# More zero products, pooled keys summed over rows, and a new order of steps in a fused attention and expert kernel

## The chip, the cores and the metric

One core of a Trainium2 chip. The metric is the device time of one execution in microseconds (us); times are medians of several runs.

## What is computed

```python
# attention: q, k, v of shape (2 batches, 8 heads, 576 tokens, 64)
out_d = sm_attn(mean of 4 tokens of q, of k, of v)        # pooled: 144 x 144 scores
out_local = softmax(q k^T / 8 where |i - j| < 4) v        # local band
x = (repeat(out_d, 4) + out_local) as 1152 tokens x 512
# experts: w1 (4, 512, 1024), w2 (4, 1024, 512)
p = domain_probs / sum(domain_probs)
out = sum over e of p[:, e] * (relu(x @ w1[e]) @ w2[e])
```

All of it is float32. The products of the experts are made of a high and a low part of each operand, three products for one.

## The kernel before

The work is cut into 1307 named steps. Each step belongs to one engine (P TensorE, V VectorE, A ScalarE, G POOL, S the load queue on SyncE), and a list written out by hand, ORDER, fixes the order in which the steps are issued. An engine does its steps strictly in that order. The dictionary ENGINE says for 133 small steps which engine does them.

Attention runs in four halves of a batch, a0 to a3, of 288 tokens each; a0 and a1 belong to the first batch. For a0, loads bring 72 x 1024 pieces of keys (k00n, k01n for the two halves of the keys), queries (q0n) and values (v00n, v01n), two loads of 288 KB each. `by_row` (k00r, q0r, k01r) reorders a piece on ScalarE or VectorE, `transposed` makes four transposes on TensorE for two heads (k00t.0 to .3, a0.qt.0 to .3, k01t.0 to .3) into one of three PSUM banks, and the steps k00te, a0.qte, k01te copy them out and free the bank. `pooled_bank` (L379 to L386, steps k00d, k01d) sums four tokens of the keys from the same bank on VectorE. The steps v00d and v01d sum the values on POOL in place.

Local attention has three blocks t in each half: a0.sc{t}.{0,1} are its scores (with products of `mask` ahead of them in a0), then max, sub, exp, sum, rec, norm on the small engines, blk (32 x 32 transposes on VectorE), pv (the product with the values), xs (sum with the pooled part), xh and xl (high and low part of x). Pooled attention goes by two pairs of groups g: ds (scores), dm (maximum), de (exponential), da, db (sum and reciprocal), dq (the share, on POOL in a0), dt (transposes), dc, dv. Its queries come from a0.qd, made on VectorE.

The first expert follows on the attention: m00 is its first 256 tokens, m00.m0 the first of eight groups of twelve products. It needs the x of all three blocks of a0 (a0.xl2 is the last) and a low part of the weights that POOL makes (wlo100). While m00 runs, attention a1 to a3 is woven into TensorE's queue; three more experts follow, with fewer products (sums of blocks in place of some of the products).

TensorE has 46 steps named warm, each with WARM[i] products of a 128 x 64 tile of zeros (`wz`) into a PSUM tile of their own (`wps`, L247), which nothing reads. Most of the 46 numbers are small or zero; their sum is 72.

Of the kernel before, what the change touches and what calls it, by code (L numbers as in the profile page):

```python
# [21 lines left out]
ORDER = """
    k00n.0 q0n.1 q0n.0 k00n.1 k00r.0 q0r.0 q0r.1 k00r.1 warm6 warm18 warm36 warm33 warm15 warm0 warm22 warm13 warm37
    warm21 warm40 k00t.0 warm11 warm29 k00t.1 warm2 warm41 warm19 warm23 a0.qt.2 warm42 a0.qt.0 warm34 a0.qt.1 warm16
    a0.qt.3 vw00 v01n.1 k01n.0 k01n.1 v00n.0 v00n.1 a1q.0 v01n.0 a1q.3 raw100 raw101 a1q.1 a1q.2 vw01 mask kstart0
    clear0 k00d.1 clear1 k00d.0 a0.start v01d.1 v00d.1 v01d.0 v00d.0 k00te.1 k00te.0 a0.qte.0 a0.qte.2 a0.qte.1
    a0.qd.0 warm27 k00t.3 k00d.3 warm5 warm17 k00t.2 k00te.3 k00te.2 a0.qte.3 a0.sc0.0 a0.sc0.1 warm12 a0.sc1.0 warm14
    a0.sc1.1 warm25 warm4 warm43 warm30 k01r.1 k00d.2 a0.qd.1 a0.max0 k01r.0 k01t.1 k01d.1 k01t.0 k01d.0 a0.max1
    a0.sub0 k01te.1 a0.sub1 k01t.2 k01d.2 warm3 a0.ds1 a0.ds0 a0.dm0 a0.dm1 k01te.0 a0.sc2.0 k01t.3 warm1 k01d.3 warm7
    a0.ds2 warm39 a0.exp0 a0.exp1 a0.de1 a0.de0 a0.da0 a0.sum1 k01te.2 a0.da1 a0.db1 a0.db0 a0.sum0 a0.dq0 a0.dt0  # L30
    warm9 a0.ds3 a0.dm2 a0.rec0 a0.dm3 k01te.3 a0.sc2.1 whi100.1 a0.dc0 a0.dq1 a0.max2 a0.de2 a0.sub2 a0.dt1 warm24
    warm28 warm38 a0.norm0 a0.da2 a0.dc1 a0.db2 a0.dq2 a0.de3 a0.exp2 a0.blk0.0 a0.da3 a0.db3 a0.blk0.1 a0.sum2
    a0.rec1 a0.dq3 a0.rec2 a0.norm1 wlo100.1 a0.blk1.1 a0.blk1.0 a0.norm2 a0.dv0 a0.dv1 a0.dt2 whi101.0 a0.dc2 a0.dt3
    a1.qt.1 warm44 a0.dv2 warm20 a0.dc3 a0.dv3 a0.pv0 whi101.1 whi100.0 a0.xd a0.xs0 a0.pv1 a1.qt.3 warm8 warm45
    warm31 a0.blk2.1 a0.blk2.0 vw02 a0.pv2 a1.qt.2 warm35 raw200 a0.xs1 k10r.3 praw raw201 k10r.2 k10r.1 a0.xh0 a0.xl0
    a1.start wlo100.0 a1.qte.1 a1.qte.3 wlo101.0 a0.xh1 whi200.1 a1.qte.2 a0.xs2 a1.qt.0 warm32 wlo101.1 whi200.0
    a0.xh2 a1.qte.0 a0.xl1 a0.xl2 a1.qd.0 a1.qd.1 warm26 a1.sc1.1 warm10 a1.sc0.1 a1.sc2.0 m00.m0 a1.ds0 a1.sc2.1
    m00.m2 m00.m3 a1.ds1 a1.dm0 m00.r0 a1.dm1 a1.madd2 wlo200.1 a1.de1 a1.de0 a1.da1 a1.da0 m00.l0 a1.sc0.0 a1.ds2
    wlo200.0 a1.db0 whi201.1 a1.dq0 a1.madd0 a1.dm2 a1.max2 a1.dt0 a1.sc1.0 a1.dc0 a1.db1 m00.r3 a1.de2 a1.da2 a1.ds3
    m00.m1 kstart1 a1.dq1 m00.r2 whi201.0 m00.r1 m00.l3 a1.max0 a1.dm3 m00.l1 a1.madd1 a1.db2 wlo201.1 a1.sub0 a1.sub2  # L40
    a1.dt1 a1.dv0 m00.m6 a1.dc1 k10r.0 m00.m4 k10t.2 a1.dv1 a1.de3 m00.r4 a1.exp0 a1.exp2 k11r.3 vw03 k11r.1 k11r.2
    vw04 vw05 k11r.0 v11n.1 v10n.1 a1.da3 a1.dq2 a1.dt2 a1.db3 m00.l2 a1.dq3 m00.m5 a1.dc2 a1.dt3 m00.o00 k10t.0
    m00.m7 a1.dc3 k10t.1 a1.dv3 a1.dv2 m00.r6 k10te.2 m00.l4 a1.sum0 wlo201.0 a1.max1 a1.sub1 a1.sum2 k11t.1 m00.o01
    m00.l6 a1.rec0 gate a1.rec2 a1.norm0 a1.blk0.0 a1.norm2 k10te.0 m00.r5 a1.exp1 a1.blk0.1 m00.l5 a1.sum1 a1.xd
    k10te.1 a1.pv0 k11te.1 a1.rec1 a1.blk2.1 a1.xs0 a1.norm1 m00.r7 a1.blk1.1 a1.blk2.0 a1.blk1.0 m00.l7 k10t.3 k11t.0
    m00.o10 k11t.3 k11t.2 m00.o02 k11te.0 a1.pv2 k11te.2 k11te.3 k11d.1 a1.pv1 a1.xs1 k10te.3 a1.xh1 a1.xl1 a1.xs2
    a1.xh0 a1.xh2 a1.xl2 a1.xl0 a2.start k10d.0 k10d.1 m00.o11 m00.o12 m00.o03 m00.g0 a2q.0 a2q.3 a2q.2 a2q.1 a2.qt.2
    m01.m0 a2.qt.1 a2.qt.0 a2.qte.1 a2.qte.0 a2.qd.0 k11d.0 v11d.1 a2.qte.2 m01.r0 m01.m1 a2.qt.3 a2.qte.3 a2.qd.1
    m00.o13 a2.ds0 a2.sc2.1 a2.sc1.0 a2.sc0.0 a2.sc0.1 a2.ds1 m00.g1 m01.m3 a2.dm1 v11n.0 a3q.3 v10n.0 a2.de1 a2.madd0
# [1321 lines left out]
```

## Time and profile before

| | us |
|---|---|
| median of 3 runs | 454.23 (452.6 to 454.64) |
| the profiled execution | 451.76 |
| its span from the first to the last instruction | 450.0 |
| TensorE busy | 440.3 (98%) |
| VectorE busy | 333.1 (74%) |
| ScalarE busy | 205.4 (46%) |
| POOL busy | 104.3 (23%) |

The span is the time between the first and the last instruction of the profiled execution; 1.76 us lie outside it. A busy share is a mean over stages with different limits. An idle time in brackets in a timeline is the wait of that engine just ahead of the row, with what ended it.

### The profile page before, as it was taken

How to read it: one execution, taken by the hardware profiler on the slowest of the kernel's cores; microseconds unless marked ns; L12 is line 12 of the kernel's file. 1: busy time of each engine (PE TensorE's matmuls, PEld its weight loads, DVE VectorE, ACT ScalarE, POOL GpSimd, SP SyncE). 2: the span in 40 equal slices, each digit the busy share in tenths (PEclk: the TensorE clock that was granted, in tenths of full speed). 3: DMA queues.
4: the chain of work that ended last, by engine and by line, in shares of the span. 5: the costliest groups of instructions: out<-in, count | busy, mean ns of one | idle time of the engine just before them, and what ended most of it. 6: DMA issues, size and time to landing. Idle time of an engine off the chain costs nothing.

```text
span 450.0 us, 10178 instructions
## 1 busy us (share of the span) xinstructions
PE 440.3 (98%) x4260; PEld 418.7 (93%) x4260; DVE 333.1 (74%) x584; ACT 205.4 (46%) x385; POOL 104.3 (23%) x125
## 2 busy tenths in 40 slices
PE   8898999999999999999999999999999999999996
PEld 8677988888988988999999999999999999999996
DVE  2789788678678796464699974667899746688983
ACT  4673541432421534454476426444664265446540
POOL 3579343361110000211341211022412110013010
PEclk9955999999999999999999999999999999999999
DMA  7998323703001010685185584054645912145135
GB/s 161 236 259 204 67 70 80 133 21 69 4 1 47 2 47 17 185 128 141 40 127 101 122 172 89 11 148 85 97 82 122 172 50 45 48 84 84 22 98 161
DMA packets 69085, 43.10 MB, mean 96 GB/s; under 512 B 27632, under 2 KB 66992, under 8 KB 69040
## 3 DMA queue, kind: packets, MB, share of 16 engines
q1 hardware_dynamic: 55392, 30.14, 25.3%
q0 software_dynamic: 13648, 12.32, 18.6%
q8 instruction: 33, 0.54, 0.5%
q14 instruction: 12, 0.10, 0.1%
HBM read 36.69 MB, written 2.36 MB: 87 GB/s over the span
## 4 chain that ended last, share of the span: by engine, by line
PE 85%; DVE 4%; issue 3%; DMA 3%; POOL 2%; ACT 1%; SPq 0%; POOLq 0%; ACTq 0%; DVEq 0%
PE ps L1021 29%; PE ps L1210 26%; PE ps L1223 4%; PE m03o L791 4%; PE m03h L766 3%; PE m01h L766 3%; PE m02h L766 3%; PE m01o L791 3%; PE m00o L791 2%; PE m00h L766 2%; DMA k00n<-in_k_dram 2%; DMA v01n<-in_v_dram 2%; PE a_qt L355 1%; PE a0pv L587 1%; DVE xs L880 1%
## 5 line engine op out<-in xcount | busy, mean ns | idle before, releaser
L1210 PE MATMUL ps<-slot,unit 128*128 128x256 f32 x1008 | 119.9, 280 | 0.2 <-DVE unit L1130 0.2
L1210 PEld LDWEIGHTS ps<-slot,unit 128*128 128x128 f32 x1008 | 119.1, 189 | 0.5 <-DVE unit L1130 0.5
L1021 PE MATMUL ps<-xhi,slot 128*128 128x288 f32 x384 | 66.5, 295 | 0.0
L1021 PE MATMUL ps<-xc,slot 128*128 128x288 f32 x432 | 60.6, 295 | 0.0
L1021 PEld LDWEIGHTS ps<-xc,slot 128*128 128x128 f32 x432 | 58.3, 188 | 0.1
L1021 PEld LDWEIGHTS ps<-xhi,slot 128*128 128x128 f32 x384 | 56.3, 188 | 0.1
L1070 POOL DMA_DIRECT2D raw<-in_moe_w_dram x15 | 19.5, 1337 | 145.2 <-DVE slot L1076 79.2
L1033 ACT ACTIVATE H<-ps 128x288 f32<-128x288 f32 x72 | 28.1, 412 | 53.8 <-PE ps L1021 53.8
L188 ACT CAST slot<-raw 128x1024 fp32r<-128x1024 f32 (+1 forms) x33 | 41.9, 1278 | 6.7 <-DVE raw L969 3.9
L1037 DVE TENSOR_TENSOR H<-H,ps 128x288 f32<-128x288 f32 x72 | 29.3, 449 | 21.1 <-PE ps L1021 21.1
L975 DVE TENSOR_TENSOR slot<-raw,slot 128x1792 fp32r<-128x1792 f32 x12 | 24.3, 2022 | 24.5 <-PE ps L1021 21.2
L1021 PE MATMUL ps<-xlo,slot 128*128 128x288 f32 x192 | 41.1, 295 | 0.0
L1125 ACT ACTIVATE unit<-H 128x1024 fp32r<-128x1024 f32 x18 | 19.1, 1063 | 28.9 <-PE ps L1210 17.4
L1121 ACT ACTIVATE unit<-H 128x512 fp32r<-128x512 f32 (+1 forms) x24 | 20.0, 844 | 25.0 <-DVE H L1037 15.4
L1108 DVE SCALAR_TENSOR_TENSOR H<-H 128x1024 f32<-128x1024 f32 (+1 forms) x18 | 28.1, 1574 | 4.0 <-ACT H L1035 3.7
L1021 PEld LDWEIGHTS ps<-xlo,slot 128*128 128x128 f32 x192 | 30.7, 188 | 0.0
L1134 DVE SCALAR_TENSOR_TENSOR unit<-H,unit 128x1024 fp32r<-128x1024 f32 x18 | 22.0, 1222 | 7.1 <-ACT unit L1125 7.0
L1076 DVE TENSOR_TENSOR slot<-raw,slot 128x1024 fp32r<-128x1024 f32 x21 | 25.3, 1217 | 2.4 <-ACT slot L188 2.4
L578 DVE STREAM_TRANSPOSE ptb<-pmb 32x256 f32<-32x256 f32 x48 | 20.8, 433 | 4.0 <-POOL pmb L574 1.4
L1130 DVE SCALAR_TENSOR_TENSOR unit<-H,unit 128x512 fp32r<-128x512 f32 (+1 forms) x24 | 22.5, 952 | 1.5 <-ACT unit L1121 1.5
L1232 DVE SCALAR_TENSOR_TENSOR acc<-ps,npr,acc 128x256 f32<-128x256 f32 x48 | 20.7, 476 | 3.3 <-PE ps L1210 3.3
...
## 6 DMA issues: line engine op xcount, KB each, us to landing
...
```

What stands on the lines that cost most here:

```text
L188: nc.scalar.copy(out_, in_)
L766: nc.tensor.matmul(ps[:, :n], w[:, d, cc:cc + P], x[:, d, n0:n0 + n], start=i == 0, stop=i == len(terms) - 1,)
L791: nc.tensor.matmul(ps[:, cs], T[f"{nm}t{f}"][:, hpart, cc:cc + P], w[:, f % 4, cs], start=f == 0 and x == 0, stop=f == KF - 1 and x == 2,)
L975: engine(f"wo{e}{i}").tensor_tensor(w1tile(i, 1), raw1(e, i), f32(w1tile(i, 0)), ALU.subtract)
L1021: nc.tensor.matmul(bank(acc_, n, i)[:, :NH // 2], w[:, d * P:(d + 1) * P], x[:, d, n * (NH // 2):(n + 1) * (NH // 2)], start=u == 0 and fi ...
L1033: nc.scalar.mul(dst, at, -1.0)
L1037: nc.vector.tensor_tensor(dst, dst, at, ALU.add)
L1076: engine(f"bo{e}{m}").tensor_tensor(w2tile(m, 1), raw2(q), f32(w2tile(m, 0)), ALU.subtract)
L1108: nc.vector.scalar_tensor_tensor(at[o], at[x], 0.0, at[y], ALU.max, op)
L1130: nc.vector.scalar_tensor_tensor(o, x, 0.0, y, ALU.max, ALU.subtract)
L1134: nc.vector.scalar_tensor_tensor(o, x, -1.0, y, ALU.mult, ALU.subtract)
L1210: nc.tensor.matmul(ps[:, t * 256:t * 256 + 256], a[:, f, t * P:t * P + P], b[:, f], start=first_ and (t, f, x) == (0, 0, 0), stop=(t, f, x ...
```

## The change

WARM is a new list with the sum 151: large numbers in the first steps.

```diff
-WARM = [13, 4, 0, 0, 0, 1, 4, 0, 0, 0, 2, 0, 0, 0, 0, 0, 1, 3, 2, 1, 0, 3, 1, 0, 1, 0, 0, 0, 0, 0, 0, 1, 0, 0, 1, 1, 0, 2, 1, 0, 19, 5, 5, 0, 0, 1]
+WARM = [14, 24, 24, 24, 10, 7, 6, 5, 5, 5, 4, 3, 2, 2, 0, 2, 2, 2, 0, 1, 1, 0, 0, 0, 0, 0, 1, 0, 0, 0, 0, 0, 0, 0, 1, 1, 1, 0, 0, 0, 2, 0, 0, 0, 2, 0]
```

The pooled keys of the second half of the keys no longer come from the PSUM banks of the transposes. POOL sums the four tokens in the untransposed rows (steps k01ds.0 and .1), TensorE transposes the sums (k01dt), and VectorE copies them out in one piece (k01de).

```diff
+    def pooled_rows(nm, src, dst, evdeps, by=1.0):
+        def rows_sum(hh):
...
+            eng.tensor_tensor(t, n[:, sl, 0:2 * D], n[:, sl, 2 * D:4 * D], ALU.add)
+            eng.tensor_tensor(o[:, sl], t[:, :, 0:D], t[:, :, D:2 * D], ALU.add)
+        def pe():
+            pt = g_tile(f"{nm}t")
+            for hp in range(HP):
+                nc.tensor.transpose(
+                    pt[:, hp * G:(hp + 1) * G], T[f"{nm}p"][:G, hp * P:(hp + 1) * P], ident[:G, :G]
+                )
...
             if b == 0:
-                pooled_bank(f"{nm}d", f"{nm}t", lambda hp, half=half: kd(half, hp, hp + 1)[:, 0], [f"kstart{b}"])
+                if nm in ('k01',):
+                    pooled_rows(f"{nm}d", f"{nm}n", lambda half=half: kd(half, 0, HP), [f"kstart{b}"])
+                else:
+                    pooled_bank(f"{nm}d", f"{nm}t", lambda hp, half=half: kd(half, hp, hp + 1)[:, 0], [f"kstart{b}"])
```

Ten small steps change their engine: to VectorE a1.norm0 and clear0 (from POOL) and k00te.3, k01te.1, k11te.3, a3.xh2 (from ScalarE); to ScalarE a2.xh0, a2.dc2, a3.xh0 and to POOL a2.xl1 (from VectorE).

ORDER is a new list. Its first steps:

```diff
-    k00n.0 q0n.1 q0n.0 k00n.1 k00r.0 q0r.0 q0r.1 k00r.1 warm6 warm18 warm36 warm33 warm15 warm0 warm22 warm13 warm37
+    warm25 warm24 warm23 warm22 warm21 k00n.1 k00n.0 q0n.1 q0n.0 k00r.0 q0r.0 q0r.1 k00r.1 warm2 k00t.0 k00t.1 a0.qt.2
+    warm3 a0.qt.0 warm20 a0.qt.1 warm40 warm19 a0.qt.3 k01n.0 v01n.1 k01n.1 k01ds.0 k01ds.1 v00n.1 v00n.0 v01n.0
```

In the load queue, the four pieces of k00n and q0n now end with a piece of the queries; k01n, v00n and v01n follow directly, then the weights raw101 and raw100, and the window of values vw00, which stood fifth, comes after two of a1's queries.

TensorE at the first scores (wps are the zero products, a0_qt and k00t the transposes of queries and keys, a0sl the scores of block 0, a0sb0 and a0sb1 those of block 1). Before:

```order
L355 MATMUL a0_qt_2_192<-ident_90,acc_89 128x72 x4
L247 MATMUL wps_131<-wz_97 64x64 x5
L355 MATMUL a0_qt_0_202<-ident_90,acc_89 128x72 x4
L247 MATMUL wps_131<-wz_97 64x64
L355 MATMUL a0_qt_1_208<-ident_90,acc_89 128x72 x4
L247 MATMUL wps_131<-wz_97 64x64
L355 MATMUL a0_qt_3_214<-ident_90,acc_89 128x72 x4
L355 MATMUL k00t_3_279<-ident_90,acc_89 128x72 x4
L247 MATMUL wps_131<-wz_97 64x64 x4
L355 MATMUL k00t_2_289<-ident_90,acc_89 128x72 x4
L501 MATMUL a0sl_297<-mask_91,ident_90 128x128 x2
```

and of the change:

```order
L247 MATMUL wps_121<-wz_97 64x64 x24
L355 MATMUL a0_qt_0_210<-ident_90,acc_89 128x72 x4
L247 MATMUL wps_121<-wz_97 64x64
L355 MATMUL a0_qt_1_216<-ident_90,acc_89 128x72 x4
L247 MATMUL wps_121<-wz_97 64x64 x3
L355 MATMUL a0_qt_3_224<-ident_90,acc_89 128x72 x4
L355 MATMUL k00t_3_294<-ident_90,acc_89 128x72 x4
L355 MATMUL k00t_2_300<-ident_90,acc_89 128x72 x4
L247 MATMUL wps_121<-wz_97 64x64 x24
L537 MATMUL a0sl_334<-mask_91,ident_90 128x128 x2
L547 MATMUL a0sl_334<-kT0_270,a0qT_285 32x32 x32
L405 MATMUL k01dt_369<-ident_90,k01dp_235 128x72 x4
```

The zero products now stand in two blocks of 24, one behind a0.qt.2 and one directly ahead of the first scores, and the transposes of the pooled keys follow the scores of block 0.

POOL from its first clears on (vw, kT, ptb and a0qT are cleared, v01n and v00n summed). Before:

```order
L221 AFFINE_SELECT canvas<-canvas 128x128
L284 MEMSET vw_219 4x512
L404 MEMSET kT_253 128x4x4
L405 MEMSET kT_253 128x4x4
L236 MEMSET ptb_92 128x1024
L236 MEMSET ptb_93 128x1024
L457 MEMSET a0qT 128x4x8
L444 TENSOR_TENSOR v01n<-v01n 72x4x128
```

and of the change:

```order
L221 AFFINE_SELECT canvas<-canvas 128x128
L399 TENSOR_TENSOR k01dt_234<-k01n 72x512
L400 TENSOR_TENSOR k01dp<-k01dt_234 72x256
L399 TENSOR_TENSOR k01dt_238<-k01n 72x512
L400 TENSOR_TENSOR k01dp<-k01dt_238 72x256
L284 MEMSET vw_251 4x512
L437 MEMSET kT_270 128x4x4
L438 MEMSET kT_270 128x4x4
L480 TENSOR_TENSOR v00n<-v00n 72x4x128
L481 TENSOR_TENSOR vd_276<-v00n 72x256
L236 MEMSET ptb_93 128x1024
```

The clear of the margins of kT, which the scores read, stands behind the two row sums of the keys; the clear of ptb_92 is on VectorE.

TensorE from the first product with the values to the first expert (a0pv0 to a0pv2, transposes of a1's queries, a1sl scores of a1, m00h0 the first group of the expert). Before:

```order
L587 MATMUL a0pv1_595<-ptb1_93,vw01_242 64x96 x8
L355 MATMUL a1_qt_3_604<-ident_90,acc_89 128x72 x4
L247 MATMUL wps_131<-wz_97 64x64 x2
L587 MATMUL a0pv2_620<-ptb0_92,vw02_615 64x96 x8
L355 MATMUL a1_qt_2_629<-ident_90,acc_89 128x72 x4
L247 MATMUL wps_131<-wz_97 64x64
L355 MATMUL a1_qt_0_667<-ident_90,acc_89 128x72 x4
L511 MATMUL a1sl_684<-kT0_253,a1qT_648 32x32 x16
L247 MATMUL wps_131<-wz_97 64x64 x2
L511 MATMUL a1sl_684<-kT0_253,a1qT_648 32x32 x32
L766 MATMUL m00h0_735<-xhi_87,wlo100_532 128x256 x4
```

and of the change:

```order
L623 MATMUL a0pv0_649<-ptb0_92,vw00_251 64x96 x8
L247 MATMUL wps_121<-wz_97 64x64 x5
L623 MATMUL a0pv1_671<-ptb1_93,vw01_259 64x96 x8
L247 MATMUL wps_121<-wz_97 64x64 x6
L355 MATMUL a1_qt_3_693<-ident_90,acc_89 128x72 x4
L623 MATMUL a0pv2_698<-ptb0_92,vw02_682 64x96 x8
L247 MATMUL wps_121<-wz_97 64x64
L355 MATMUL a1_qt_2_708<-ident_90,acc_89 128x72 x4
L355 MATMUL a1_qt_0_744<-ident_90,acc_89 128x72 x4
L247 MATMUL wps_121<-wz_97 64x64 x10
L547 MATMUL a1sl_771<-kT0_270,a1qT_726 32x32 x16
L247 MATMUL wps_121<-wz_97 64x64 x2
```

Five, six and ten zero products stand between these groups, and 48 products of scores (a1sl) in place of 32 come directly ahead of m00h0.

## Rows read from the trace of the kernel before

**Rows 1.** The page's second part: TensorE's granted clock in 40 slices, tenths.

```profile
PEclk9955999999999999999999999999999999999999
```

**Rows 2.** Stages (us): busy time of PE, PEld, DVE, ACT, POOL; granted clock, DMA share, GB/s.

```profile
20.00:25.00 5.00, 4.36 (x62) 3.46 (x62) 3.29 (x13) 3.77 (x12) 4.54 (x6) 0.75 1.05 373
...
40.00:45.00 5.00, 5.00 (x116) 4.49 (x117) 5.00 (x8) 2.06 (x3) 5.00 (x6) 0.50 0.58 127
45.00:50.00 5.00, 5.00 (x71) 4.41 (x70) 3.21 (x10) 2.73 (x10) 0.86 (x2) 0.86 0.72 144
...
100.00:200.00 100.00, 99.80 (x906) 90.70 (x905) 74.19 (x137) 37.46 (x78) 10.09 (x10) 1.00 0.25 56
```

**Rows 3.** TensorE's timeline, first expert and pooled scores: start, duration, operation, count.

```profile
42.83 1.22 PE L766 MATMUL m00h<-xhi,wlo 128*128 128x256 f32 x4
...
45.69 1.02 PE L658 MATMUL a1sd<-kd,a1qd 64*72 64x144 f32 x8
...
46.94 0.74 PE L766 MATMUL m00h<-xhi,wlo 128*128 128x256 f32 x4
...
48.47 0.64 PE L766 MATMUL m00h<-xhi,wlo 128*128 128x256 f32 x4
...
50.27 0.71 PE L658 MATMUL a1sd<-kd,a1qd 64*72 64x144 f32 x8
```

**Rows 4.** VectorE's timeline, from the maximum of block 2 to a1's pooled queries.

```profile
26.65 0.49 DVE L545 TENSOR_REDUCE a0mx<-a0sl 128x4 f32<-128x128 f32 x2 [0.79 <-PE a0sl L511]
...
30.49 2.33 DVE L574 TENSOR_TENSOR pmb<-pmb,a0sm 128x256 f32<-128x256 f32 x1
...
34.67 0.68 DVE L574 TENSOR_TENSOR pmb<-pmb,a0sm 128x256 f32<-128x256 f32 x1
...
43.80 1.40 DVE L374 TENSOR_REDUCE a1qd<-a1qT 128x144 f32<-128x576 f32 x2
```

**Rows 5.** TensorE's timeline: zero products at full and at half clock.

```profile
10.15 0.80 PE L247 MATMUL wps<-wz 128*64 128x64 f32 x10
...
12.39 0.33 PE L247 MATMUL wps<-wz 128*64 128x64 f32 x2
...
22.66 1.12 PE L247 MATMUL wps<-wz 128*64 128x64 f32 x8
```

**Rows 6.** ScalarE's timeline: copies behind the loads of queries and keys.

```profile
8.16 1.05 ACT L188 COPY acc<-q0n 72x1024 f32<-72x1024 f32 x1 [2.03 <-DMA q0n<-in_q_dram]
9.67 1.04 ACT L188 COPY acc<-k00n 72x1024 f32<-72x1024 f32 x1 [0.46 <-DMA k00n<-in_k_dram]
```

**Rows 7.** POOL's timeline: clears, sums of values, low part of weights.

```profile
2.12 0.51 POOL L284 MEMSET vw<- 4x512 f32 x1
...
2.67 1.83 POOL L236 MEMSET ptb<- 128x1024 f32 x2
...
12.37 1.27 POOL L444 TENSOR_TENSOR v01n<-v01n 72x512 f32<-72x512 f32 x1 [7.79 <-DMA v01n<-in_v_dram]
13.72 0.72 POOL L445 TENSOR_TENSOR vd<-v01n 72x256 f32<-72x256 f32 x1
...
20.64 1.26 POOL L444 TENSOR_TENSOR v01n<-v01n 72x512 f32<-72x512 f32 x1 [0.30 <-DMA v01n<-in_v_dram]
...
29.75 2.79 POOL L321 TENSOR_TENSOR wlo<-raw,whi 128x256 fp32r<-128x256 f32 x4
```

**Rows 8.** TensorE's timeline in the first attention half.

```profile
11.33 0.47 PE L355 MATMUL a_qt<-ident,acc 72*128 72x72 f32 x4 [0.39 <-ACT kT L188]
...
14.57 0.66 PE L501 MATMUL a0sl<-mask,ident 128*128 128x128 f32 x4
...
16.99 0.76 PE L511 MATMUL a0sb<-kT,a0qT 64*32 64x32 f32 x64
...
19.40 1.23 PE L658 MATMUL a0sd<-kd,a0qd 64*72 64x144 f32 x8 [0.75 <-DVE a0mx L545]
...
25.43 0.70 PE L710 MATMUL a0pdt<-ident,a0pd 72*72 72x72 f32 x4 [0.21 <-POOL a0pd L702]
```

More of the change, by code (lines that the diff above doesn't have):

```diff
@@ L26 @@
[L26 to L30, printed above, removed]
@@ L36 @@
[L36 to L40, printed above, removed]
@@ L41 @@
[L41 to L49, printed above, removed]
-    a2.dm0 a2.de0 a2.ds2 m01.m2 a2.sc2.0 a2.sc1.1 a2.ds3 m01.m6 a2.da1 m01.l0 a2.da0 a2.max0 a2.db0 m01.r3 m01.r1
@@ new lines @@
+    a0.max1 a0.sub1 k00d.2 a0.sub0 k01te.1 k01t.2 warm16 a0.ds1 a0.ds0 a0.dm0 a0.dm1 k01te.0 a0.sc2.0 warm8 k01t.3
+    warm14 a0.ds2 a0.exp0 a0.exp1 a0.de0 a0.de1 a0.sum1 k01te.2 a0.da0 a0.da1 a0.db0 a0.sum0 a0.db1 a0.dq0 warm9
+    a0.dt0 a0.ds3 a0.dm2 a0.dm3 a0.rec0 k01te.3 a0.sc2.1 whi100.1 a0.dc0 a0.dq1 a0.max2 a0.de2 a0.sub2 warm15 a0.dt1
+    warm26 a0.norm0 a0.da2 a0.dc1 a0.db2 a0.dq2 a0.de3 a0.exp2 a0.blk0.0 a0.da3 a0.db3 a0.blk0.1 a0.sum2 a0.rec2
+    a0.rec1 a0.dq3 a0.norm1 wlo100.1 a0.blk1.1 a0.blk1.0 a0.norm2 a0.dv0 warm13 a0.dv1 warm17 a0.dt2 warm34 whi101.0
@@ new lines @@
+    a0.dc2 warm10 a0.dt3 a1.qt.1 warm12 a0.dv2 a0.dc3 a0.dv3 a0.pv0 whi100.0 whi101.1 a0.xd a0.xs0 a0.blk2.1 warm7
+    a0.pv1 a0.blk2.0 vw02 warm6 a1.qt.3 a0.pv2 warm35 a1.qt.2 raw200 a0.xs1 raw201 praw k10r.2 k10r.1 a0.xh0 a0.xh1
+    a0.xl0 a1.start wlo100.0 a1.qte.1 a1.qte.3 wlo101.0 a0.xs2 whi200.1 a1.qte.2 a1.qt.0 wlo101.1 whi200.0 a0.xh2
+    a1.qte.0 a0.xl1 a0.xl2 a1.qd.0 a1.qd.1 warm11 warm5 a1.sc1.1 warm44 a1.sc0.1 a1.sc2.1 a1.sc2.0 m00.m0 a1.ds0
+    a1.sc0.0 m00.m3 m00.m2 a1.ds2 a1.ds1 m00.r0 a1.dm1 a1.dm0 a1.madd2 wlo200.1 a1.de1 a1.de0 a1.da1 a1.da0 m00.l0
@@ new lines @@
+    m00.o13 m01.m1 a2.ds0 a2.sc2.1 a2.sc1.0 a2.sc0.1 a2.sc0.0 m01.m3 a2.ds1 m00.g1 a2.dm1 v11n.0 a3q.3 v10n.0 a2.de1
+    a2.madd0 a2.dm0 a2.de0 a2.ds2 m01.m2 a2.sc1.1 a2.sc2.0 a2.ds3 m01.m6 a2.da1 m01.l0 a2.da0 a2.max0 a2.db0 m01.r1
+    m01.r3 a2.dq0 v10d.0 v10d.1 m01.r2 a2.db1 a2.dq1 m01.l1 a2.dm2 m01.l2 a2.dt0 m01.m4 a2.dt1 a2.madd1 a2.max1 a2.dc0
+    a2.de2 a2.da2 m01.l3 a2.sub1 a3q.2 v11d.0 vw10 a3q.1 a3q.0 vw11 vw12 m01.r4 a2.madd2 m01.l4 a2.db2 a2.exp1 a2.max2
+    a2.dm3 a2.sub2 a2.de3 a2.dc1 m01.m5 m01.o10 m01.r5 a2.dq2 m01.l5 m01.r6 m01.l6 a2.sum1 a2.da3 a2.db3 a2.dq3
@@ L484, in pooled_of @@
         def pooled_of(h):
[L485 removed]
+            keys_ = [x for i in range(2) for x in ([f"k0{i}de"] if f"k0{i}" in ('k01',) else [f"k0{i}d.{2 * h + u}" for u in range(2)])] if b == 0 else [f"k1{i}d.{h}" for i in range(2)]
             return [f"{a}.qd.{h}"] + keys_
```

115 lines of the change are left out of this document (68 added, 47 removed).

## The prediction

> **What bounds the kernel now.** I read the views from the outside in. The page's clock line first: TensorE's granted clock is full for the first two slices, at half for the next two, full to the end [rows 1]. So the kernel loses something between 22 and 46 us, in the first attention block, and nothing afterwards. Then the table by stages: TensorE's busy time is 4.36 of 5 us and the clock 0.75 in 20 to 25 us, 5.00 at 0.50 in 40 to 45, and 99.80 of 100 us at 1.00 from 100 to 200 [rows 2]. A mean of 0.75 over 20 to 25 puts the fall at 22.5 us, one of 0.86 over 45 to 50 the return at 46.4. From about 43 us on, TensorE is a full queue. What happens ahead of that moves the end one for one; what happens later on other engines is hidden by the queue.
>
> So I ask what brings TensorE to the point where the queue is full. That is the first product of the first expert (m00.m0) and the pooled scores a1.ds0 behind it, which start at 42.83 and 45.69 us and end at 46.71; the return of the clock falls into that [rows 2, 3]. The price of the half clock stands in the same rows: the twelve products of a group take 2.86 us (42.83 to 45.69) at half and 1.53 us (46.94 to 48.47) at full; the pooled scores 1.02 against 0.71 [rows 3].
>
> Then VectorE, which feeds these. From 30.49 us to 45.20 us (43.80 + 1.40) the timeline has thirteen lines, and none shows an idle time ahead of it; the first and the last stand in [rows 4]. a1.ds0 needs the pooled queries that VectorE ends at 45.20. **Consequence:** with the same VectorE work at the same times, a full clock lets a1.ds0 end at 45.20 + 0.71 = 45.91 in place of 46.71. The clock alone is worth 0.8 us there, not the 13 us that 26 us at half clock suggest, because VectorE and not TensorE sets the pace.
>
> **The change, part by part.**
>
> *Loads and copies at the start.* Loads of 288 KB land about 1.5 us apart (8.16, then 9.67) [rows 6]. The last of the first four is now a half of the queries, and ScalarE has two copies of 1.04 us behind it where it had one: the copies of keys start at 11.75 in place of 10.71, and a0.qt.0, which needs a PSUM bank that they free, at 12.4 in place of 11.33 [rows 6, 8]. Cost: 1.0 us.
>
> *Zero products.* A record costs (0.80 - 0.33) / 8 = 0.059 us at full clock, two records to a product; eight records last 1.12 at half [rows 5]. 24 products are 48 records, 2.8 us. The first 24 behind a0.qt.2 end at about 12.1: free, because of the wait just named. The next 24 stand ahead of the first scores. Before, that stretch was 14.57 - 11.33 = 3.24 us long [rows 8], with four zero products in it that are now gone (0.5 us); it now ends at 12.4 + 2.7 = 15.1. With 2.8 us of zero products and 0.6 of mask products the scores start at 18.5. Without them they would wait for POOL's clear of the keys' margin: that stands behind the new row sums, of which the second needs the seventh load (9.67 + 3 x 1.5 = 14.2) and 2.07 us (12.37 to 14.44) [rows 7], and a clear of 0.5 [rows 7]: 16.9. So these 24 cost 1.6 us. Bounds: nothing, if POOL is 1.6 us later than that, and 2.8.
>
> *Pooled keys by rows.* Four VectorE reductions of about 0.4 us become one copy; POOL gets 4.1 us of adds, TensorE four transposes (0.4). The keys are ready at about 20.2. TensorE reaches a0.ds0 only behind the second block's scores (0.66 for the mask and 0.76 [rows 8]), ten zero products (1.2), three transposes (1.0) and two more products: 18.5 + 0.8 + 0.4 + 1.4 + 1.2 + 1.0 + 0.3 = 23.6, and it ends at 24.3 where it ended at 20.63 [rows 8]. The earlier keys buy nothing.
>
> *Values.* The last load of values is now the tenth, 9.67 + 6 x 1.5 = 18.7, where POOL got it at 20.64 [rows 7]. POOL does four pairs of 2.07 and a clear of 0.9 [rows 7] from 16.9: free at 26.1. What comes next on it is a0.dq0, and behind that a0.dt0 on TensorE. Lower bound for a0.dt0: 26.1 and an operation of 0.7, or 26.8. Upper bound: as far behind the pooled scores as before, 25.43 - 20.63 = 4.8, or 29.1 [rows 8]. Those 4.8 contain POOL's wait for the late values, which is gone; in their place stand five zero products of 0.6 directly ahead of a0.dt0. I take 27.4, near the lower end: 2.0 us late. From a0.dt0 to VectorE's maximum of block 2 it was 26.65 - 25.43 = 1.22 us [rows 4, 8], all TensorE at half clock; at the ratio of [rows 3], 1.53 / 2.86, it is 0.7. So the maximum starts at 28.1 in place of 26.65: **1.5 us late** (0.9 to 3.2 by the bounds).
>
> *VectorE's stretch.* The same operations follow, so all to 45.20 moves to 46.7. In it one normalisation takes 2.33 us, the same on the next block 0.68 [rows 4]; the long one overlaps POOL's four pieces of 2.79 us and ends 0.3 after them [rows 7]. Both move by the same 1.5 us, so I keep the 2.33. [...]
>
> *First expert.* a1.ds0 ends at 46.7 + 0.71 = 47.4 in place of 46.71: 0.7 late. One group of local scores (0.3) now stands ahead of it that stood behind: -0.3. Everything behind is the same full queue at the same clock.
>
> *Engines changed later* (the normalisation of a1's block 0 on VectorE, 0.68, and eight others): nothing, because TensorE's queue covers them; in 100 to 200 us it idles 0.2 us [rows 2]. Without that cover 0.7.
>
> **Sum:** +0.7 - 0.3 = **+0.4 us**. The profiled execution took 451.76 us (span 450.0), so 452.2; the median of the three runs is 454.23, which gives **454.6 us**. A measurement of this kernel can tell about 0.5%, 2.3 us.
>
> **Rivals.**
>
> *A. The clock falls again in the waits for VectorE.* Before, it fell at 22.5 us after a stretch of small products with a wait of 0.75 us in it [rows 8]. The changed order has waits of that size and larger: between the first and the second a0.pv VectorE works some 2.9 us (a normalisation of 2.33 and transposes) and the table gives five zero products, 0.6 us; the next wait gets six. For it: these waits. Against it: TensorE is denser up to there. If it falls at 35 to 39 us, m00.m0 and a1.ds0 lose 0.5 (a part is hidden behind VectorE), and each of the next two groups 1.33, until the clock is back; before, it came back only at 46.4, with TensorE busy without a gap from 40 on [rows 2]. Price: +0.4 + 0.5 to +0.4 + 0.5 + 2.7, or +0.9 to +3.6, middle +2.4: **456.6**. It decides from the first m00 group that runs at half clock behind 47 us.
>
> *B. The start is shorter than I make it, and the normalisation doesn't stall.* The zero products may fall in waits after all (-1.6), and if block 1 is normalised ahead of POOL's burst it takes 0.68 (-1.65). Together with +0.4: -2.85, **451.4**; one of the two alone, -1.2. For it: POOL's burst and VectorE's instruction are less than 1 us apart in both programs. Against it: by my chain both move alike. [...]
>
> *C. The change doesn't do what it says*: the clock falls before 30 us as now. Then the chain's 2.0 us stay and the zero products run at 0.13 a record: +2 to +4. It is the upper end of A and I count it there.
>
> **How the numbers follow.** The forecast 0.38 (between 453.4 and 455.9), A with C 0.30, B 0.32. Faster by over 0.5% needs both halves of B (0.7 of it, 0.22) or a tail of the forecast (0.02): 0.24. Slower by over 0.5% is 0.6 of A (0.18) and 0.05 from the forecast, where the start is worse: 0.23. The rest, 0.53, is within. The range takes B down to 451.2 and A up to 457.3; some 0.08 lies outside at either end.
>
> **What would show it.** Right: granted clock 1.00 from 20 to 50 us; a0.sc0.0 at about 18, a0.dt0 at 27 to 28; the normalisation of block 1 over 2 us; a1.ds0 ending at about 47.4; from there the same rows as before. Wrong: half clock in 35 to 48 (A), or a1.ds0 ending before 45.5 (B). If a1.ds0 ends where I say and the time still differs by over 1.5 us, a stall behind 47 us that I count as covered is the cause.

## The result, and the profile after

The changed kernel takes 460.86 us (median of six runs, 458.66 to 461.69) against 454.29 us beside it: 1.0143 times, 95% interval 1.0109 to 1.0177. The forecast was 454.6 us with a range up to 457.3, so it was wrong. Kernels built on the changed one scatter by up to 12 us from run to run (their mean granted clock between 0.97 and 1.00); their medians are over all runs, their ratios leave out the runs over 1.5% above the fastest.

The page's clock line of the changed kernel has fewer slices at half than [rows 1]:

```profile
PEclk9979999999999999999999999999999999999999
```

The stages, with the columns of [rows 2]:

```profile
20.00:25.00 5.00, 2.95 (x62) 2.69 (x57) 1.87 (x8) 0.00 (x0) 4.60 (x6) 0.84 0.79 196
25.00:30.00 5.00, 5.00 (x63) 4.08 (x62) 2.47 (x7) 2.75 (x11) 0.00 (x0) 0.50 0.78 151
40.00:45.00 5.00, 1.03 (x14) 1.06 (x16) 4.86 (x8) 0.17 (x1) 4.92 (x8) 0.89 0.38 85
45.00:50.00 5.00, 5.00 (x68) 4.62 (x65) 4.79 (x10) 2.90 (x5) 2.66 (x4) 0.77 0.04 9
100.00:200.00 100.00, 99.77 (x916) 89.73 (x915) 74.64 (x146) 37.84 (x86) 14.15 (x18) 1.00 0.16 43
```

The clock is better, and yet TensorE works 2.95 of the 5 us from 20 on, and 1.03 of the 5 us from 40 on. TensorE's timeline says where the holes are (start, duration, operation, count, idle time ahead):

```profile
18.09 0.76 PE L547 MATMUL a0sl<-kT,a0qT 64*32 64x32 f32 x64
...
19.67 0.72 PE L547 MATMUL a0sb<-kT,a0qT 64*32 64x32 f32 x61
22.44 0.25 PE L547 MATMUL a0sb<-kT,a0qT 64*32 64x32 f32 x3 [2.05 <-issue]
...
24.34 1.70 PE L355 MATMUL k01t<-ident,kr 72*128 72x72 f32 x12
...
43.97 1.55 PE L623 MATMUL a0pv<-ptb,vw 128*64 128x96 f32 x16 [4.86 <-issue]
...
53.45 0.71 PE L694 MATMUL a1sd<-kd,a1qd 64*72 64x144 f32 x8
...
55.08 0.28 PE L547 MATMUL a1sl<-kT,a1qT 64*32 64x32 f32 x12 [0.67 <-issue]
...
95.53 0.65 PE L694 MATMUL a2sd<-kd,a2qd 64*72 64x144 f32 x6 [1.03 <-issue]
```

Three holes are odd: TensorE stops inside a group of like products, whose operands are all there (61 of 64 records, then 2.05 us of nothing; 20 of 32; 2 of 8). The 4.86 us at 43.97 are of another kind, though the view names no releaser for them either: these products read what VectorE's four transposes at 42.09 write, and VectorE is late. Its timeline, and POOL's:

```profile
33.10 0.49 DVE L581 TENSOR_REDUCE a0mx<-a0sl 128x4 f32<-128x128 f32 x2 [0.60 <-PE a0sl L547]
...
37.12 4.93 DVE L610 TENSOR_TENSOR pmb<-pmb,a0sm 128x256 f32<-128x256 f32 x1
42.09 1.78 DVE L614 STREAM_TRANSPOSE ptb<-pmb 32x256 f32<-32x256 f32 x4
43.90 0.42 DVE L610 TENSOR_TENSOR pmb<-pmb,a0sm 128x256 f32<-128x256 f32 x1
...
51.27 1.41 DVE L374 TENSOR_REDUCE a1qd<-a1qT 128x144 f32<-128x576 f32 x2
```

```profile
36.20 2.79 POOL L321 TENSOR_TENSOR wlo<-raw,whi 128x256 fp32r<-128x256 f32 x4
...
39.01 8.64 POOL L321 TENSOR_TENSOR wlo<-raw,whi 128x256 fp32r<-128x256 f32 x12
```

The normalisation of block 1 takes 4.93 us where it took 2.33 [rows 4].

**What the end depends on.** a1.ds0 (the a1sd row at 53.45) ends at 54.16 where it ended at 46.71 [rows 3]. From there to the end of the span it is 403.3 us before (450.0 - 46.71). After it is 459.4 - 54.16 = 405.2, of which the two later stops take 1.70. In all sixteen experiments below it is 402.5 to 403.6 once the stops behind a1.ds0 are taken off. So nearly the whole difference is made ahead of 55 us, plus those stops: 7.45 + 1.70 of the 9.4 us between the two spans.

### The profile page after: what moved, and what is told of

It reads as the page before. It is cut to its first block, busy times and chain, and to the rows that moved or that the text cites. A ratio compares the mean times of both kernels' runs of the same rounds, so it can differ in the third digit from the quotient of the medians.

```text
span 459.4 us, 10513 instructions
## 1 busy us (share of the span) xinstructions
PE 445.1 (97%) x4422; PEld 425.1 (93%) x4422; DVE 335.1 (73%) x583; ACT 204.1 (44%) x384; POOL 105.1 (23%) x128
## 4 chain that ended last, share of the span: by engine, by line
PE 94%; DVE 2%; issue 2%; ACT 1%; POOL 0%; POOLq 0%; DVEq 0%; ACTq 0%
PE ps L1057 29%; PE ps L1246 26%; PE wps L247 5%; PE ps L1259 4%; PE m03h L802 4%; PE m03o L827 4%; PE m01h L802 3%; PE m02h L802 3%; PE m01o L827 2%; PE m02o L827 2%; PE m00h L802 2%; PE m00o L827 2%; PE a_qt L355 1%; DVE ptb L614 1%; PE a0pv L623 1%
## 5 line engine op out<-in xcount | busy, mean ns | idle before, releaser
L1106 POOL DMA_DIRECT2D raw<-in_moe_w_dram x15 | 19.5, 1337 | 142.0 <-DVE slot L1112 77.4
L1073 DVE TENSOR_TENSOR H<-H,ps 128x288 f32<-128x288 f32 x72 | 29.5, 451 | 15.9 <-PE ps L1057 12.3
L1144 DVE SCALAR_TENSOR_TENSOR H<-H 128x1024 f32<-128x1024 f32 (+1 forms) x18 | 28.1, 1576 | 4.3 <-ACT H L1071 4.0
L1157 ACT ACTIVATE unit<-H 128x512 fp32r<-128x512 f32 (+1 forms) x24 | 20.0, 845 | 23.6 <-DVE H L1073 13.6
L247 PE MATMUL wps<-wz 128*64 128x64 f32 x302 | 25.5, 249 | 1.0 <-DVE wz L196 1.0
L247 PEld LDWEIGHTS wps<-wz 128*64 128x64 f32 x302 | 23.1, 161 | 2.2 <-DVE wz L196 1.0
```

Source lines behind the costliest of these rows:

```text
L247: nc.tensor.matmul(T["wps"][:64, :64], wz, wz, start=True, stop=True)
L1073: nc.vector.tensor_tensor(dst, dst, at, ALU.add)
L1144: nc.vector.scalar_tensor_tensor(at[o], at[x], 0.0, at[y], ALU.max, op)
```

## Experiments on the stops

**Where they fall.** Records counted up to each stop, by stages that begin at 0 (busy time and count of PE, then of PEld):

```profile
0.00:20.41 20.41, 19.40 (x351) 18.32 (x351) 8.97 (x28) 8.04 (x9) 10.55 (x21) 1.00 0.82 228
0.00:54.43 54.43, 46.38 (x854) 41.92 (x854) 33.65 (x84) 22.84 (x46) 29.31 (x48) 0.91 0.73 184
0.00:94.52 94.52, 84.95 (x1356) 75.54 (x1357) 67.04 (x165) 39.75 (x97) 43.51 (x70) 0.95 0.57 140
```

With the semaphore instructions in TensorE's queue (2, 20 and 39 by then) that is 704, 1728 and 2752 instructions: 1024 apart to the last one. The page's DMA part has a queue for instructions, and its first part TensorE's counts:

```profile
PE 445.1 (97%) x4422; PEld 425.1 (93%) x4422; DVE 335.1 (73%) x583; ACT 204.1 (44%) x384; POOL 105.1 (23%) x128
...
q8 instruction: 35, 0.57, 0.5%
```

35 packets of 16 KB for some 8,900 TensorE instructions is 255 each. My theory R, a reading of these counts (the trace has the packets and not what asks for them): a piece of 256 is asked for when the one ahead of it is begun, and TensorE stops if it runs through that one before the next can be used. I call the first instruction of a piece a border; 704, 1728 and 2752 are 192 and a multiple of 256. In the changed kernel's trace the packets of the first seven borders, 192 to 1728, start 0.1 to 6.4 us behind them. Here the border ahead of the first stop, at instruction 448, is passed with the first scores, at 18.12 us; the packet starts at 20.03 and takes 0.93; TensorE goes on at 22.44, 1.5 us after it. Score products are short (64 records with their loads, 128 instructions, in 0.76 us), so the 256 instructions between the borders lasted 2.3 us, and the refill, from the border until TensorE goes on, 4.3; for the second stop it was 4.15 (50.93 to 55.08), the figure of the expectations below. By the same count the other two stops ended 1.5 and 1.6 us behind a packet.

Three runs shift the borders without touching the work: very small zero products (64 x 32) in place of some of the first block, while TensorE waits for the first load.

```diff
-        for _ in range(n):
+        for _ in range(7 if i == 0 else n):
             nc.tensor.matmul(T["wps"][:64, :64], wz, wz, start=True, stop=True)
+        for k in range(57 if i == 0 else 0):
+            j, c = k % 4, 64 + 32 * (k // 4 % 14)
+            nc.tensor.matmul(
+                T["wps"][32 * j:32 * j + 32, c:c + 32], wz[:64, :32], wz[:64, :32], start=True, stop=True
+            )
```

> The changed kernel with 50 more, very small zero products in the first block of zero products, where TensorE waits for the first load anyway; four instructions each, so every later TensorE instruction stands 200 places later. Theory R (refill): TensorE's program reaches it in 16 KB pieces of 256 instructions, each asked for when the one before is begun, and 4.15 us pass until it can be used; the three stops of the changed kernel (2.05, 0.67 and 1.03 us) stand at its instructions 704, 1728 and 2752, 1024 apart. Shifted by 200, no 256 instructions between two such borders take less than 4.15 us: no stop inside the a0sb, a1sl or a2sd products, time 3.5 to 5 us under the changed kernel's, 456 to 457.5. Rival P (place): the stops belong to these products or to the loads in flight at these times; then they stay where they are, within 0.3 us, and the time stays at 460 to 461.5.

> As the run before, with 64 more small products: 256 instructions, one whole piece. Theory R: the borders fall on the same products as in the changed kernel, so the stops come back: about 2 us after 61 of the 64 records of a0sb, 0.5 to 0.9 in a1sl, 0.8 to 1.2 in a2sd, time 459.5 to 462. Rival P says the same of this run, but also of the one with 50; a rival by which small products ahead cure the stops in themselves (by a busier or warmer TensorE) says no stops here and 456 to 457.5.

 (71 in place of 57.)

> The kernel before with 28 more small zero products in its first block, 112 instructions. Theory R, worked out from the trace of before: at this shift 256 instructions up to the first k01t products take only 2.7 us and 256 up to the second half of a2's scores only 1.7 us; stops of about 1.4 us near 18 us and of about 2.5 us near 84 us, time 3 to 5 us over the kernel before, 457 to 459. Rival P: no stop, 453.5 to 455.

 (The kernel before, 7 and 34.)

With 50 more, TensorE's timeline has no stop in any of the three places:

```profile
21.21 0.76 PE L552 MATMUL a0sb<-kT,a0qT 64*32 64x32 f32 x64
...
23.21 0.97 PE L360 MATMUL k01t<-ident,kr 72*128 72x72 f32 x12
...
40.54 1.55 PE L628 MATMUL a0pv<-ptb,vw 128*64 128x96 f32 x16 [4.85 <-issue]
```

Its profiled run took 454.8 us, 6.5 under the changed kernel's 461.27, though the small products delay the start by 1.5. The median of ten runs is 459.8 (ratio 1.0117, 1.0084 to 1.0151): the wait for VectorE stays, and in most runs the clock falls more than in the profiled one. The medians alone (459.8 and 460.86) therefore don't tell what the stops cost; the profiled runs do. With 64 more, the stops are back at the same products, and one more is there:

```profile
11.40 2.72 PE L247 MATMUL wps<-wz 128*64 128x64 f32 x43 [1.12 <-issue]
...
27.63 0.32 PE L552 MATMUL a0sb<-kT,a0qT 64*32 64x32 f32 x3 [5.11 <-issue]
...
58.82 0.28 PE L552 MATMUL a1sl<-kT,a1qT 64*32 64x32 f32 x12 [0.45 <-issue]
...
99.47 0.65 PE L699 MATMUL a2sd<-kd,a2qd 64*72 64x144 f32 x6 [1.20 <-issue]
```

The median of that run is 461.09; two of its four runs took 457 us, two 465 and 466, and the profile is of one of these two, so the 5.11 us are shown for that one alone. The ratio, of the two lower runs, is 1.0075 (1.0049 to 1.0102). The kernel before, with 28 more, got one of the two stops that R foresaw:

```profile
87.08 0.26 PE L516 MATMUL a2sl<-kT,a2qT 64*32 64x32 f32 x7 [1.21 <-issue]
```

and took 456.47 (1.0058, 1.0037 to 1.0080). So an idle piece of code at the start puts a stop at 86 us. The border is shown: in the traces of eight of the runs here TensorE stops inside a group of like products, and each time at 192 and a multiple of 256 (448, 704, 960, 1728, 1984, 2496, 2752 and 3008 occur). The fixed 4.15 us is not shown: the 5.11 is longer, and the first stop that R foresaw for the kernel before did not come. Nor does a packet always start behind its border: in the changed kernel's trace the one of the border at 1984 starts at 63.47 us, ahead of the border itself at 64.56; why so early is open.

**What sets their length.** From a border to the start of its packet some time passes: for the border at 448 it was 1.9 us in the changed kernel, and 3.4 (20.90 to 24.28) in the run with 14 products fewer, below. For the changed kernel's border at 1216 it was 6.4 (38.66 to 45.03), without a stop, since TensorE then took 12.3 us for its 256 instructions. In the run with the stop of 5.11 us, TensorE went on 7.4 us behind the border (20.24 to 27.63). The next run takes data out of the packet's way.

```diff
-    raw101 raw100 a1q.0 a1q.1 vw00 a1q.3 a1q.2 vw01 mask
+    a1q.0 a1q.1 vw00 a1q.3 a1q.2 vw01 raw101 raw100 mask
```

> The changed kernel with the loads of the two first weight blocks (2 x 1 MB) put behind the queries of a1 and the first two values on SP's queue; TensorE's instructions are the same, so the borders of 256 are at the same products. Theory Q (the refill waits in the DMA engines behind data): the request of the border at the first scores, which waited 1.9 us for its packet to start in the changed kernel, waits another time than before (0.5 to 1.2 us if the weights are what it stood behind), and the stop in a0sb falls to 0.5 to 1.5 us; the time falls by 0.5 to 3 us, unless the weights now come late for the first expert. Rival: the 4.3 us from border to use are fixed: stop 1.9 to 2.1 us as before.

```profile
20.63 0.25 PE L547 MATMUL a0sb<-kT,a0qT 64*32 64x32 f32 x3 [0.75 <-issue]
```

The time from the border at 448 to its packet fell from 1.9 to 0.2 us and the stop from 2.05 to 0.75, with the data moved between 18 and 20 us down from 306 to 82 GB/s. Behind this shorter stop TensorE keeps its speed (the twelve k01t transposes take 0.97 us, not 1.70). The stop at 2752 is as it was, 1.02 us. The time (458.77; 1.0125, 1.0092 to 1.0159) gained little: the late weights hold up ScalarE, and TensorE waits 5.15 us for it. In these traces the crossing of a border is hidden where its 256 instructions outlast the refill (12.3 us at the border at 1216), and costs 0.45 to 5.11 us where they don't (the stop of 2.05, with 2.3 us against 4.3).

## Experiments on the normalisation

```diff
-'a0.norm1': 'V'
+'a0.norm1': 'G'
```

> The changed kernel with the normalisation of block 1 of a0 on POOL, ahead of POOL's pieces of wlo, in place of VectorE. Theory N: the 4.93 us of that instruction on VectorE (0.42 for the same work on the next block) are a wait for POOL's pieces, which follow each other without a gap; on POOL it takes about 1.5 us, VectorE's next transposes start about 3 us earlier, and the time falls by 2.5 to 4 us, to 457 to 458.5; the three stops of TensorE stay. Rival: the wait passes to the next normalisation or to whatever VectorE has next, since POOL's pieces are still to come: within 1 us of the changed kernel's 460.9.

> The kernel before with the normalisation of block 1 on POOL, nothing else. Theory N: the 2.33 us on VectorE become some 0.6 us on POOL; VectorE's stretch up to a1's pooled queries ends 1.5 to 2 us earlier, TensorE's stretch behind it too: 451 to 452.5 against 453.4 to 454.3. Rival: POOL's burst of wlo now starts 0.6 us later and the wait passes on; within 0.7 us of the kernel before.

In the changed kernel: 459.02 us over ten runs. Four of them lie between 450.6 and 456.7, and the ratio of 1.0013 (0.9976 to 1.0050) is of these; six, the profiled one among them, lie between 457.4 and 462.3. In the profiled run the 4.93 us are gone (0.62 on POOL, VectorE's next transposes wait 0.73 us), but the stop in a0sb is there (2.10), TensorE runs at half clock from 24 to 44 us behind it, and a1.ds0 ends at 54.52. One cause alone was not enough in most runs. In the kernel before it is **449.75 us, 0.9890 times (0.9849 to 0.9931), under both kernels**: POOL takes the normalisation ahead of its pieces, and a1.ds0 ends at 44.45 in place of 46.71.

```profile
31.52 0.62 POOL L574 TENSOR_TENSOR pmb<-pmb,a0sm 128x256 f32<-128x256 f32 x1 [0.73 <-DMA vw<-in_v_dram]
32.09 2.97 POOL L321 TENSOR_TENSOR wlo<-raw,whi 128x256 fp32r<-128x256 f32 x4
```

Why 2.33 and 4.93: in both traces the instruction ends 0.3 us behind a piece of POOL's that a pause follows. Before, it ended at 32.82, and POOL idled 0.40 us for ScalarE's high part of the weights behind its first four pieces:

```profile
32.99 12.86 POOL L321 TENSOR_TENSOR wlo<-raw,whi 128x256 fp32r<-128x256 f32 x16 [0.40 <-ACT whi L188]
```

In the changed kernel that part was ready, POOL went straight on (the row at 39.01), and VectorE waited through a second four. Its instruction ends at 42.05, 0.3 us behind POOL's eighth piece, where the trace has a pause of 0.08 us (41.76 to 41.84).

The part was ready because the new ORDER swaps two steps, of which the prediction says nothing. POOL's second four pieces (wlo100.0) need whi100.0. The kernel before has `whi101.1 whi100.0` on ScalarE, so that whi100.0 is the second of the two casts, and the change has `whi100.0 whi101.1`. Before, and of the change:

```profile
30.92 1.99 ACT L188 CAST whi<-raw 128x1024 fp32r<-128x1024 f32 x2
```

```profile
37.12 1.99 ACT L188 CAST whi<-raw 128x1024 fp32r<-128x1024 f32 x2
```

Before, the second cast ends at 32.91 and POOL goes on behind it. In the change the first ends at 38.16, ahead of POOL's 39.01. That POOL came later doesn't explain it, since ScalarE's casts moved by 6.2 us and POOL's pieces by 6.45. No run here has the swap alone. The runs agree on the pause: 4.92 and 4.94 us where POOL does not pause behind its first four (50 more products; no blocks, below), 2.33 with a pause of 0.39 (the kernel before with blocks), and the late weights make one in the changed kernel:

```profile
37.88 2.13 DVE L610 TENSOR_TENSOR pmb<-pmb,a0sm 128x256 f32<-128x256 f32 x1
```

```profile
36.95 2.77 POOL L321 TENSOR_TENSOR wlo<-raw,whi 128x256 fp32r<-128x256 f32 x4
...
40.86 9.80 POOL L321 TENSOR_TENSOR wlo<-raw,whi 128x256 fp32r<-128x256 f32 x12 [1.07 <-ACT whi L188]
```

One of POOL's pieces takes 0.70 us (2.79 / 4). For block 1 every run that has both at work shows three to seven times that (2.13 to 4.94 us). The normalisation of block 2 runs inside the same stretch of POOL's pieces (34.67 us before [rows 4], 43.90 in the change) and takes 0.42 to 0.70 us, no more than one piece. Why block 1 waits longer is open.

## Both causes together

```diff
-WARM = [14, 24, 24, 24, 10,
+WARM = [0, 24, 24, 24, 10,
```

> The changed kernel with 14 zero products fewer in its first block (56 instructions less: for the borders of 256 the same as the 200 more of the run with 50 small products, but nothing added ahead of the loads) and the normalisation of block 1 on POOL. If stops (theory R) and the wait for POOL's pieces (theory N) are the two things that the forecast missed, both are gone: no stop in a0sb, a1sl, a2sd; no VectorE instruction of over 2 us from 30 to 45 us; the clock at 1.00 to 50 us; time 448.5 to 452, which is under both kernels. Rival C: the clock falls all the same in TensorE's waits for VectorE; then the time is 453 to 457.

> The changed kernel with 50 small zero products more at the start (borders shifted by 200) and the normalisation of block 1 on POOL: both causes taken away, all blocks of zero products kept. If they are the whole miss: no stop, no VectorE wait of over 1 us for POOL's pieces, clock 1.00 to 50 us, and the forecast's 454.6 less the 2 us that it kept for the normalisation and plus the 1.5 us that the small products cost at the start, 452 to 455. Rival: the clock still falls in TensorE's waits: 456 to 460.

 (The 57 small products and 'G'.)

The first, with 'G' too, took 457.32 (450.6 to 461.2; ratio 0.9962, 0.9921 to 1.0004). Its stop did not vanish but moved to another product at the same count:

```profile
26.99 0.66 PE L355 MATMUL k01t<-ident,kr 72*128 72x72 f32 x7 [2.34 <-issue]
```

```profile
0.00:24.66 24.66, 21.53 (x351) 20.20 (x351) 10.61 (x34) 7.99 (x10) 14.03 (x25) 0.86 0.83 221
```

351 records again: the count decides, not the product. I had taken the refill for 4.15 us; here its packet alone started 3.4 us behind the border. The second took 455.0 (0.9961, 0.9928 to 0.9995), with one stop of 1.99 at 44.62 in its profile; its runs lie between 450.2 us at a mean clock of 1.00 and 460.5 at 0.978. So with the wait for POOL's pieces and the stop at the scores gone, the changed kernel comes down to 450 to 452 where the clock stays up (five of the twelve runs); what decides whether it does stays open.

## Experiments on the zero products and the pooled keys

Without the blocks of 24 (the normalisation on VectorE, then on POOL); with the first block kept; with seven products fewer ahead of k01t; and with blocks put into the kernel before:

```diff
-WARM = [14, 24, 24, 24, 10,
+WARM = [8, 0, 0, 0, 10,
```

The run with seven fewer has 15 and 3 in place of 8 and 10 there; the one with the first block kept has 48 small products in place of the 8, and 24 in the third place. All but the first of these have 'G'. In the kernel before, which keeps 'V', WARM 40 and 42 go from 19 and 5 to 22 and 24, and a new block of 24 stands ahead of the scores:

```diff
-    a0.sc0.0 a0.sc0.1
+    warm46 a0.sc0.0 a0.sc0.1
```

> The changed kernel with 78 of the zero products ahead of the first scores taken out (24 of its first block and 6 more there, and the two blocks of 24 behind the first load and ahead of the scores), nothing else: the run without blocks, but with the normalisation of block 1 on VectorE as the change has it. If the normalisation's wait for POOL and the zero products are the two separate causes, this run lies over the run without blocks (451.5) by the wait, 4.93 less 0.7, so 455 to 456, and under the changed kernel (460.9) by the rest, 5 us. Rival: without the blocks POOL's pieces and the normalisation meet otherwise and the wait is gone: 451 to 453.

> As the run with 14 fewer zero products and the normalisation on POOL, and the three blocks of 24 zero products ahead of the first scores taken out too (78 products fewer than the changed kernel, 312 instructions: the same place of the borders). The forecast put 1.6 us of the first scores' delay on these blocks. Theory Z (they cost time and do nothing): the first scores start 1.5 to 4 us earlier, the clock stays up as without the stops, and the time is 0.5 to 2 us under that run. Rival W (they keep the clock up): without them the clock falls to half between 20 and 25 us as in the kernel before, and the time is over that run's by 1 to 4 us.

> A version meant to be under both: the changed kernel with the normalisation of block 1 on POOL and without the two blocks of 24 behind the first load and ahead of the scores, but with the zero products ahead of the first load kept (14 of them as 48 small ones, so that the borders of 256 fall as in the run without blocks). In the run without blocks TensorE's products from 7.5 to 23 us took 0.74 where 0.47 is usual, after 4.2 us without work. If that came from the missing products at the start, they take 0.47 here, the first scores start near 16 us and the time is 448.5 to 450.5. Rival: POOL's clear of the keys' margin sets the first scores anyway (17.5 us): 450.5 to 452.

> The run without blocks with 3 in place of 10 zero products ahead of the first k01t transposes and 7 more at the start, where TensorE waits for the load (so the borders stay). These 20 records took 2.39 us there. If they cost time: the first pooled scores start 1 to 1.7 us earlier, time 450 to 451. Rival: the transposes wait for ScalarE's copy of the keys anyway (0.5 us of such a wait was seen): within 0.5 us of 451.5.

> The kernel before with blocks of zero products as the changed one has them, nothing else: 24 behind a0.qt.2 (5 stood there), 24 ahead of the first scores (none stood there), 3 more at the start. Forecast's rule (each product has its price and nothing comes back but the clock): the first scores start 4 to 5 us later than 14.57, the chain behind them comes 2 to 4 us later where no wait hides it, time 455 to 458 if the clock falls at 22 us anyway. Rival W (they keep the clock up and so pay for themselves): clock 1.00 to 30 us, time 451.5 to 454. By theory R the 184 instructions more put no border where 256 pass in under 4 us: no stop.

| run | median, us | ratio (interval) | a1.ds0 ends | half speed, us |
|---|---|---|---|---|
| no blocks, VectorE | 456.61 | 1.0073 (1.0044 to 1.0102) | 52.01 | to 22, 41 to 46 |
| no blocks, POOL | 451.48 | 0.9939 (0.9912 to 0.9965) | 46.57 | to 23 |
| first block kept | 451.65 | 0.9960 (0.9940 to 0.9980) | 46.35 | 11 to 23 |
| seven fewer | 456.09 | 1.0034 (1.0005 to 1.0062) | 51.63 | 9 to 42 |
| before with blocks | 457.16 | 1.0089 (1.0062 to 1.0117) | 51.70 | 27 to 51 |

Only the first of these had a stop, at instruction 448:

```profile
23.96 0.66 PE L355 MATMUL k01t<-ident,kr 72*128 72x72 f32 x7 [0.48 <-issue]
```

The expectation for "seven fewer" took these 0.5 us for a wait for ScalarE's copy; TensorE stops there behind five of twelve like products. Without the blocks the kernel lies 3 to 4 us under the changed one (by the ratios and by the medians), and POOL's normalisation is worth another 5 to 6. Together the two steps lead from 460.86 to 451.48 us, with all ten runs of the second within 3 us. So the blocks cost more than the 1.6 us of the forecast. That they do it by the borders that they shift is argued: no run here takes them out and leaves every border, but with all of them kept, 50 small products more and 'G', five runs took 450.2 to 452.4, no more than without blocks. In the old order they cost 3.9 us (453.27 beside them) and the clock still fell. But the ten products ahead of k01t pay: with three, TensorE stays at half speed until 42 us in the profiled run, and the median is 4.6 us longer (three of its twelve runs took 451.5 to 453.0 all the same). "They cost time" was wrong for those. The first block doesn't matter here (451.65 us with it, 451.48 without): TensorE waits 2.76 us for ScalarE behind it and falls to half speed anyway (four transposes take 0.47 us ahead of the wait and 0.74 behind it).

The pooled keys, from the banks again, and by rows in the kernel before:

```diff
-    a0.qt.3 k01n.0 v01n.1 k01n.1 k01ds.0 k01ds.1
+    a0.qt.3 k01n.0 v01n.1 k01n.1
...
-    k01t.1 a0.max1 a0.sub1 k00d.2 a0.sub0 k01te.1 k01t.2 warm16
+    k01t.1 k01d.1 k01d.0 a0.max1 a0.sub1 k00d.2 a0.sub0 k01te.1 k01t.2 k01d.2 warm16
...
-    k01t.3 warm14
+    k01t.3 k01d.3 warm14
```

In the kernel before:

```diff
-    v01d.1 v00d.1
+    v01d.1 k01ds.0 k01ds.1 v00d.1
...
-    k01t.1 k01d.1 k01t.0 k01d.0 a0.max1
+    k01t.1 k01t.0 k01dt k01de a0.max1
...
-    k01d.2
...
-    k01d.3
```

> As the run with 14 fewer zero products and the normalisation on POOL, with the pooled keys of the second half taken from the PSUM banks by four VectorE reductions again (two of its zero products come back, so that the instructions up to the scores differ by no more than 8 from that run). Forecast: the earlier keys buy nothing, within 0.7 us of that run. Rival: the four reductions stand in VectorE's work ahead of the first pooled scores, 4 x 0.41 us less one copy of 0.46, and everything behind moves: 0.8 to 1.6 us slower.

> The run without blocks (451.5, runs within 3 us) with the pooled keys of the second half from the PSUM banks again. Forecast: the earlier keys buy nothing: 450.8 to 452.2. Rival: VectorE's four reductions of 0.41 to 0.45 us stand ahead of the first pooled scores in place of one copy of 0.46, and TensorE waits for them: 452.3 to 454.

> The kernel before with the normalisation of block 1 on POOL (449.75) and the pooled keys of the second half summed over rows on POOL, two pairs of 2.0 us between the sums of the values. Rival G (gain): the 0.75 us that TensorE waits for VectorE ahead of the first pooled scores vanish: 448.5 to 449.5. Forecast (nothing gained, and POOL is later for the values by 4 us, of which it idled little): 450 to 453.

The first, from the run with 14 products fewer, took 460.7 (1.0128, 1.0076 to 1.0180); the second, from the run without blocks, 461.28 (1.0172, 1.0141 to 1.0202), **9.8 us over it**. Its timeline:

```profile
25.89 0.74 PE L355 MATMUL k01t<-ident,kr 72*128 72x72 f32 x4 [1.67 <-ACT kT L188]
...
31.29 0.74 PE L355 MATMUL k01t<-ident,kr 72*128 72x72 f32 x4
```

TensorE waits 1.67 us for ScalarE's copy of the keys, which had waited for VectorE's reduction from the same bank, and 0.57 once more, and stays at half speed until 48 us. The kernel before with row sums took 450.13 (0.9921, 0.9896 to 0.9946) against 449.75 without them: nothing gained there. So their worth depends on the order around them; how much of the 9.8 comes from the place that I gave the reductions is open.

## Why the prediction was wrong, step by step

- **Right:** the full queue behind a1.ds0 (402.5 to 403.6 us in every run). The first scores came at 18.09 for 18.5, in part by luck: the 1.0 us that the loads were to cost did not come (the copies of keys start at 10.63, before at 10.62, and not at 11.75), while the block of 24 behind a0.qt.2, called free, held a0.qt.0 back from 11.33 to 11.92.
- **"granted clock 1.00 from 20 to 50 us" (failed):** from the first scores to VectorE's maximum of block 2 the chain, at full clock and with no wait of TensorE for its own instructions, has 28.1 - 18.5 = 9.6 us. With the stop it is 33.10 - 18.09 = 15.0; with 50 more products, no stop and full clock it is 10.0. So the stop cost 2.05 and, by that comparison, the half clock behind it 2.9. No term of the sum was a wait of TensorE for its own instructions, and the zero products that shift its borders were priced by their duration alone. The condition of rival C came (the clock was at half from 23.4 to 30.2 us), for a reason not in it, but its price of 2 to 4 us, counted into A, was too small: 6.6 by the medians. A's sign came too (half again from 43.9 to 47.3, behind the wait of 4.86 us), though the first m00 group, at 51.84, ran at full clock.
- **"Both move by the same 1.5 us, so I keep the 2.33" (failed):** 4.93, so 2.60 more. The 2.33 was not a price but the length of POOL's run up to a pause that ScalarE's cast made, and the change's own ORDER moves that cast ahead of its neighbour: the pause was gone. VectorE's work from there to the pooled queries of a1 took 10.63 us in place of 12.38. a1.ds0, now behind m00.m0 on TensorE, began 0.77 after them, and 0.2 went ahead of the normalisation, so 0.8 came back.
- **"Everything behind is the same full queue" (failed in part):** two stops, 1.70 us.
- **Sum for a1.ds0:** 47.4 - 0.4 (first scores) + 2.05 + 2.9 + 0.4 (10.0 in place of 9.6) + 2.6 - 0.8 = 54.15; measured 54.16. With the stops behind, 8.5 of the 9.1 us between 452.2 and the profiled 461.27. The sum is made of differences between runs, so that it closes is less of a proof than the runs that take out a cause each.
- **"The earlier keys buy nothing":** so in the old order (0.4 us between two runs). In the new one the keys from the banks, as I placed them, were 9.8 us slower. The zero products, priced at 1.6 us, cost more in blocks (3.9 us in the old order), while the ten ahead of k01t save 4.6 in the new one.
- **Slips that decide nothing:** two zero products net, not four, are gone ahead of the first scores; the 26 us at half clock are 23.9 by the prediction's own marks (22.5 to 46.4); the middle of +0.9 and +3.6 is +2.25.
